# Cosine attention, then a GELU feed-forward, on one core: the opening of the program as one list in another order, and one quad's row sums on VectorE

## The chip, the cores and the metric

One core of a Trainium2 chip. The time is the device time of one execution in microseconds; the kernel before was run three times, at 400.53, 400.88 and 407.3 us, median 400.88. One more execution was recorded by the hardware profiler. Its span, from the first to the last instruction, is 398.6 us; start times below count from the span's start.

The engines are named as the profile names them: PE is TensorE (matmuls; PEld is its weight loading), DVE is VectorE, ACT is ScalarE, POOL is GpSimd, SP is SyncE, which here only issues DMAs. Every engine works through its own instructions in program order and waits on semaphores for the others.

## The reference

Two stages: attention with normalised queries and keys (8 batches, 12 heads, 448 positions, 64 wide), then a feed-forward with exact GELU on the 3584 rows that result (768 to 2048 to 768).

```python
q_n = q / (norm(q, axis=-1) + 1e-06)
k_n = k / (norm(k, axis=-1) + 1e-06)
scores = q_n @ k_n.T / tau                      # tau = 0.1
attn = exp(scores - max)                        # rows divided by their sum
o = (attn / (sum(attn, axis=-1) + 1e-09)) @ v
x = o.transpose(0, 2, 1, 3).reshape(3584, 768)
h = x @ w_in
out = (0.5 * h * (1 + erf(h / sqrt(2)))) @ w_out
```

Since the rows are normalised, scores lie between -10 and 10 and the kernel subtracts no maximum.

## The kernel before

Everything is done by **quads**: four heads of one batch. A batch has three quads, so quad g belongs to batch g // 3, counted from zero; quad 3 is the first of the second batch. A quad's two head pairs are indexed s, its seven chunks of 64 keys c. The preparation of a quad is a **unit**; quad 0 is split into units 0 and 1 (one head pair each), so for later quads unit u is quad u - 1.

The steps of a quad, each a small function in the kernel:

- `load_qk(g)`: q and k from HBM, two DMAs on SP's queue; a pool of four tiles. `load_v`, `load_wi` and `load_wo` load v, w_in and w_out on POOL's queue and turn them into bfloat16 on the way.
- `square`, `reduce`, `logs`, `roots`, `inverses`: the reciprocal norms. Squares on ACT or POOL, sums along a row on DVE, a square root on ACT as logarithm and exponential, the reciprocal on DVE.
- `scale`: q and k times their reciprocal norm, to bfloat16, on POOL.
- `transposes`: the scaled tile turned, by seven PE transposes into PSUM with a DVE copy behind (`copies`) in the opening, later by one DMA transpose on SP's queue.
- `scores(g, banks, p)`: key-by-query scores of two chunks (or of one chunk for both head pairs) in a pair of PSUM banks, four matmuls of 64x64. `exps`: their exponential on ACT, 128x896. `visit(p)` is the next scores and exponential in line, on PSUM pair p.
- `sums(g)`: the row sums of the probabilities as matmuls with ones. `folded` and `gathered` do the same for other quads as additions of the chunks on POOL or DVE; `turned_all` and `inverted_all` finish them with DVE transposes. `turned`, `inverted`: the same for `sums`. `spread`: the reciprocal sums laid out along the rows.
- `values(g)`: probabilities times v. `normalise`: times the spread reciprocals, into x, the input of the feed-forward, one of its six column blocks per call.
- `w_in`: one of the sixteen projection tiles hp of a batch, six matmuls of 128x128 on 448 columns, one for each column block of x; then GELU on ACT into g. Quad 2's `normalise` writes the last two of the six blocks.
- `second_pieces`: the matmuls of the output tiles op, handed out one by one ("pieces", sixteen to a tile) between the scores of the next batch; a DVE copy and a store end each tile.

The order of the instructions is written out by hand for each engine at once: the functions are called in the order wanted, with `tc.manual_schedule()`. `attention_first` is the list for batch 0, `first(b)` the projections of batch b, `attention(b, fill)` the attention of batch b with the output pieces of the batch before (`run()` hands out as many as `parts` says). `upto(f, n)` calls a loading or preparing step up to number n. `spin(n)` issues n matmuls that nobody reads, into the bank that the next tile will take.

ACT holds one set of functions at a time: logarithm and exponential in one, GELU in another; a table load stands between them. PSUM has eight banks: two or three pairs for scores, values and projections (`ps_st`, `third`), two single ones that alternate (`ps_mm`, `mm_tile`), and during batch 0 two more for sums and values (`ps_acc`).

One copy only orders the loads: `late` is a copy on POOL that reads the last element of quad 0's k, so that POOL's loads of v and w_in are issued after quad 0 has landed.

Of the kernel before, what the change touches and what calls it, by code (L numbers as in the profile page):

```python
# [9 lines left out]
F32 = mybir.dt.float32  # L10
# [6 lines left out]
def kernel(  # L17
# [246 lines left out]

    def gathered(g, p):
# [58 lines left out]
    def values(g, chunks=range(C), p=None):  # L324
        for c in chunks:
            if c == 0 and g < NQ:
# [70 lines left out]
    def second_pieces(sb, t, ni):  # L397
        state = {}

        def mm(kf):  # L400
# [8 lines left out]
            if kf == KF - 1:  # L409
                nc.vector.tensor_copy(ot[:, ni * NH:(ni + 1) * NH], ps[:, :NH])  # L410
# [7 lines left out]
        return [lambda kf=kf: mm(kf) for kf in range(KF)]  # L418
# [46 lines left out]
    early = {}  # L465

# [5 lines left out]
    def attention_first():  # L472
        x_t[0] = xp.tile([128, KD, S], BF16, tag="x", name="x0")
        DV, AC, GP = nc.vector, nc.scalar, nc.gpsimd
        Q, K = 0, 1
        square(0, ((AC, Q),))
        square(0, ((AC, K),))
        reduce(0, Q)
        reduce(0, K)
        square(1, ((AC, Q),))  # L480
        upto(load_v, 1)
        logs(0)
        reduce(1, Q)
        roots(0)
        upto(load_wi, 1)
        square(1, ((AC, K),))
        inverses(0)
        square(2, ((AC, Q),))
        reduce(1, K)
        scale(0, ((GP, 1),))  # L490
        logs(1)
        reduce(2, Q)
        roots(1)
        scale(0, ((GP, 0),))
        spin(2)
        transposes(0, 1)
        square(2, ((AC, K),))
        inverses(1)
        spin(1)
        transposes(0, 0)  # L500
        square(3, ((AC, Q),))
        copies(0, 1)
        scale(1, ((GP, 0),))
        copies(0, 0)
        square(3, ((AC, K),))
        scale(1, ((GP, 1),))
        upto(load_qk, 5)
        spin(1)
        transposes(1, 0)
        reduce(2, K)  # L510
        scores(0, ((0, 0), (0, 1)))
        upto(load_v, 2)
        transposes(1, 1)
        copies(1, 0)
        logs(2)
        scores(0, ((0, 2), (0, 3)))
        roots(2)
        upto(load_wi, 2)
        exps(0, ((0, 0), (0, 1)))
        inverses(2)  # L520
        copies(1, 1)
        exps(0, ((0, 2), (0, 3)))
        spin(2)
        scores(0, ((0, 4), (0, 5)))
        scale(2, ((GP, 0),))
        reduce(3, Q)
        exps(0, ((0, 4), (0, 5)))
        spin(1)
        scores(0, ((1, 0), (1, 1)))
        reduce(3, K)  # L530
        exps(0, ((1, 0), (1, 1)))
        spin(1)
        scores(0, ((1, 2), (1, 3)))
        scale(2, ((GP, 1),))
        upto(load_qk, 6)
        transposes(2, 0)
        exps(0, ((1, 2), (1, 3)))
        sums(0, (0,))
        copies(2, 0)
        scores(0, ((1, 4), (1, 5)))  # L540
        logs(3)
        scores(0, ((0, 6), (1, 6)))
        roots(3)
        transposes(2, 1)
        exps(0, ((1, 4), (1, 5)))
        inverses(3)
        sums(0, (1,))
        scale(3, ((GP, 0),))
        copies(2, 1)
        sums(0, (2,))  # L550
        exps(0, ((0, 6), (1, 6)))
        sums(0, range(3, 5))
        scores(1, ((0, 0), (1, 0)))
        scores(1, ((0, 1), (1, 1)))
        sums(0, (5,))
        exps(1, ((0, 0), (1, 0)))
        sums(0, (6,))
        upto(load_wi, 3)
        transposes(3, 0)
        turned(0)  # L560
        exps(1, ((0, 1), (1, 1)))
        scores(1, ((0, 2), (1, 2)))
        values(0, (0,))
        scale(3, ((GP, 1),))
        upto(load_wi, 4)
        copies(3, 0)
        values(0, (1,))
        exps(1, ((0, 2), (1, 2)))
        values(0, (2,))
        scores(1, ((0, 3), (1, 3)))  # L570
        inverted(0)
        values(0, range(3, 5))
        spread(0, 1)
        values(0, (5,))
        exps(1, ((0, 3), (1, 3)))
        scores(1, ((0, 4), (1, 4)))
        values(0, (6,))
        spread(0, 0)
        sums(1, (0,))
        square(4, ((GP, K),))  # L580
        exps(1, ((0, 4), (1, 4)))
        sums(1, (1,))
        scores(1, ((0, 5), (1, 5)))
        normalise(0, 0)
        transposes(3, 1)
        exps(1, ((0, 5), (1, 5)))
        scores(1, ((0, 6), (1, 6)))
        copies(3, 1)
        sums(1, (2,))
        square(4, ((GP, Q),))  # L590
        square(5)
        upto(load_wo, 2)
        exps(1, ((0, 6), (1, 6)))
        sums(1, range(3, 5))
        normalise(0, 1)
        scores(2, ((0, 0), (1, 0)))
        sums(1, (5,))
        exps(2, ((0, 0), (1, 0)))
        sums(1, (6,))
        scores(2, ((0, 1), (1, 1)))  # L600
        turned(1)
        values(1, range(2))
        exps(2, ((0, 1), (1, 1)))
        values(1, (2,))
        scores(2, ((0, 2), (1, 2)))
        inverted(1)
        values(1, range(3, 5))
        spread(1, 0)
        values(1, (5,))
        exps(2, ((0, 2), (1, 2)))  # L610
        values(1, (6,))
        scores(2, ((0, 3), (1, 3)))
        sums(2, (0,))
        reduce(4, K)
        normalise(1, 0)
        exps(2, ((0, 3), (1, 3)))
        sums(2, (1,))
        scores(2, ((0, 4), (1, 4)))
        spread(1, 1)
        values(2, (0,))  # L620
        sums(2, (2,))
        exps(2, ((0, 4), (1, 4)))
        scores(2, ((0, 5), (1, 5)))
        normalise(1, 1)
        values(2, range(1, 3))
        exps(2, ((0, 5), (1, 5)))
        values(2, (3,))
        scores(2, ((0, 6), (1, 6)))
        exps(2, ((0, 6), (1, 6)))
        reduce(4, Q)  # L630
        spin(1)
        early[4] = mm_tile("hp0_4")[:, :S]
        w_in(0, early[4], 4, range(2))
        sums(2, range(3, 7))
        values(2, (4,))
        logs(4)
        turned(2)
        values(2, (5,))
        roots(4)
        values(2, (6,))  # L640
        inverted(2)
        inverses(4)
        scale(4)
        spread(2, 1)
        spread(2, 0)
        normalise(2, 1)
        normalise(2, 0)
        done.update({square: 6, reduce: 5, root: 5, scale: 5, transposes: 5})

# [49 lines left out]

    def attention(b, fill):
        fill = list(fill)
        if b == 1:
            parts = iter((20, 13, 14, 17, 16, 16))
        elif b == 2:
            parts = iter((22, 12, 12, 13, 11, 13, 11, 11, 11, 6, 6))
        elif len(fill) == 128:
# [31 lines left out]
        if b == 1:  # L740
            upto(scale, u + 3)
            upto(load_v, b + 2)
            upto(transposes, u + 3)
            upto(load_qk, g0 + NQ + 2)
            upto(square, u + 4)
            visit(0, 1, 2)
            run()
            visit(0, 1, 2)
            run()
            upto(load_qk, g0 + NQ + 3)  # L750
            visit(0, 1)
            upto(square, u + 5)
            run()
            visit(0, 1, 2)
            both(g0, 0)
            upto(load_v, b + 3)
            upto(load_qk, g0 + NQ + 4)
            visit(1, 2)
            upto(reduce, u + 4)
            run()  # L760
            visit(1, 2, 0)
            both(g0 + 1, 1)
            visit(2, 0)
            logs(6)
            roots(6)
            run()
            both(g0 + 2, 2)
            inverses(6)
            done[root] = 7
        elif b == 2:  # L770
            upto(scale, u + 3)
            upto(load_qk, g0 + 6)
            upto(transposes, u + 3)
            upto(scale, u + 4)
            upto(load_qk, g0 + 7)
            upto(transposes, u + 4)
            visit(0, 1, 2)
            run()
            visit(0, 1, 2)
            norms(9)  # L780
# [230 lines left out]
```

## Time and profile before

| what | value |
|---|---|
| three runs | 400.53, 400.88, 407.3 us; median 400.88 |
| the profiled execution | span 398.6 us, mean granted PE clock 0.999 |
| busy | PE 392.0, POOL 250.6, DVE 264.0, ACT 267.8 us |
| first transposes of quad 0 on PE | 8.65 us |
| exponentials of quads 0, 1, 2 | 12.29 to 31.22 us, 21 of them |
| projections of batch 0 | 32.65 to 51.33 us, with 14 transposes of quad 3 between |
| attention of batch 1 with the output pieces of batch 0 | 51.33 to 79.15 us |
| projections of batch 1 | 79.15 to 97.44 us |
| attention of batch 2 | 97.44 to 133.45 us |
| loads of quads 4 and 5 issued on SP | 11.29 and 16.60 us |
| DMA transposes of quads 4 and 5 issued on SP | 46.34 and 51.47 us |

A busy time is the time in which an engine had an instruction in work; PE's instructions overlap, so a busy PE isn't one at its peak. The chain of waits goes back from the last instruction: at each step to what released it, or to the instruction before it on the same engine. In a row of a timeline the first number is the start, the second the length, then engine, line, operation, output and inputs, shape and count; in brackets stands the idle time before it and who ended it.

### The profile page before, as it was taken

How to read it: one execution, taken by the hardware profiler on the slowest of the kernel's cores; microseconds unless marked ns; L12 is line 12 of the kernel's file. 1: busy time of each engine (PE TensorE's matmuls, PEld its weight loads, DVE VectorE, ACT ScalarE, POOL GpSimd, SP SyncE). 2: the span in 40 equal slices, each digit the busy share in tenths (PEclk: the TensorE clock that was granted, in tenths of full speed). 3: DMA queues.
4: the chain of work that ended last, by engine and by line, in shares of the span. 5: the costliest groups of instructions: out<-in, count | busy, mean ns of one | idle time of the engine just before them, and what ended most of it. 6: DMA issues, size and time to landing. Idle time of an engine off the chain costs nothing.

```text
span 398.6 us, 8027 instructions
## 1 busy us (share of the span) xinstructions
PE 392.0 (98%) x3245; PEld 207.8 (52%) x3245; DVE 264.0 (66%) x530; ACT 267.8 (67%) x399; POOL 250.6 (63%) x162
## 2 busy tenths in 40 slices
PE   7999999999999999999999999999999999999996
PEld 3444555555545555555555555555555555555564
DVE  5787214955487999589963999769973797461021
ACT  6995787557988877888665977889656756504300
POOL 5898814269699694959587394969768391920000
PEclk9999999999999999999999999999999999999999
DMA  8999999747296890678145591566024720130033
GB/s 290 261 258 217 205 233 308 154 106 226 50 254 234 158 230 2 178 150 207 70 105 138 126 240 38 162 113 147 2 27 101 148 46 2 41 77 3 1 80 80
DMA packets 66485, 54.52 MB, mean 137 GB/s; under 512 B 38672, under 2 KB 62352, under 8 KB 66448
## 3 DMA queue, kind: packets, MB, share of 16 engines
q1 hardware_dynamic: 54464, 41.79, 39.0%
q0 software_dynamic: 11600, 11.80, 18.8%
q8 instruction: 25, 0.41, 0.4%
q10 hardware_dynamic: 384, 0.43, 0.3%
q14 instruction: 12, 0.10, 0.1%
HBM read 45.61 MB, written 11.01 MB: 142 GB/s over the span
## 4 chain that ended last, share of the span: by engine, by line
PE 95%; issue 1%; DVE 1%; POOL 1%; ACT 0%; POOLq 0%
PE hp L469 37%; PE op L406 36%; PE st L242 9%; PE o L320 4%; PE o L335 4%; PE op L425 1%; PE sm L305 1%; PE sh L667 1%; PE tp L221 1%; PE sm L314 1%; PE spin L463 0%; POOL wi L441 0%; DVE nq L168 0%; POOL qkb L204 0%; POOL v L145 0%
## 5 line engine op out<-in xcount | busy, mean ns | idle before, releaser
L252 ACT ACTIVATE pt<-st 128x896 bf16<-128x896 f32 x155 | 132.5, 916 | 29.0 <-PE st L242 28.4
L406 PE MATMUL op<-wo,g 128*128 128x384 bf16 x864 | 148.1, 326 | 0.0
L469 PE MATMUL hp<-x,wi 128*128 128x448 bf16 x768 | 147.0, 353 | 0.1
L204 POOL TENSOR_TENSOR qkb<-qk,rn 128x896 bf16<-128x896 f32 (+1 forms) x50 | 80.2, 1628 | 66.3 <-DVE rn L188 64.9
L406 PEld LDWEIGHTS <-g 128*128 128x128 bf16 x864 | 81.4, 98 | 62.6 <-issue 11.2
L469 PEld LDWEIGHTS <-wi 128*128 128x128 bf16 x768 | 74.4, 98 | 71.1 <-issue 2.8
L263 POOL TENSOR_TENSOR acc<-acc,pt 128x896 f32<-128x896 f32 x55 | 103.8, 1887 | 4.3
L929 ACT ACTIVATE g<-hp 128x448 bf16<-128x448 f32 x128 | 63.6, 552 | 63.6 <-PE hp L469 63.5
L410 DVE COPY ot<-op 128x384 f32<-128x384 f32 x54 | 29.9, 555 | 83.1 <-PE op L406 80.8
L168 DVE TENSOR_REDUCE nq<-sq 128x14 f32<-128x896 f32 (+1 forms) x50 | 50.6, 1038 | 10.2 <-POOL sq L160 6.7
L242 PE MATMUL st<-qkT 64*64 64x448 bf16 x620 | 46.0, 356 | 0.2 <-ACT pt L252 0.2
L160 POOL TENSOR_TENSOR sq<-qk 128x896 f32<-128x896 f32 x18 | 29.9, 1683 | 16.3 <-DMA qk<-in_q_dram 10.9
L369 DVE TENSOR_TENSOR x<-o,rs 128x448 bf16<-128x448 f32 x48 | 28.0, 609 | 9.9 <-PE sh L667 6.4
L270 DVE TENSOR_TENSOR acc<-acc,pt 128x896 f32<-128x896 f32 x30 | 33.0, 1099 | 1.0
L158 ACT ACTIVATE sq<-qk 128x896 f32<-128x896 f32 (+1 forms) x32 | 27.8, 902 | 2.2 <-DMA qk<-in_q_dram 1.8
L364 DVE STREAM_TRANSPOSE rs<-rc 128x448 f32<-128x448 f32 x48 | 28.7, 626 | 0.6
L242 PEld LDWEIGHTS <-qkT 64*64 64x64 bf16 x620 | 17.9, 105 | 20.5 <-issue 12.7
L263 POOL TENSOR_TENSOR acc<-pt 128x896 f32<-128x896 bf16 x11 | 20.7, 1879 | 8.9 <-DVE x L369 8.9
L320 PE MATMUL o<-pt,v 64*64 64x448 bf16 x364 | 24.2, 351 | 0.0
L673 ACT ACTIVATE pt<-sh 128x448 bf16<-128x448 f32 x26 | 14.1, 544 | 9.2 <-PE sh L667 8.5
L276 DVE STREAM_TRANSPOSE ta<-acc 128x448 f32<-128x448 f32 x32 | 18.5, 617 | 0.2
L335 PE MATMUL o<-pt,v 64*64 64x448 bf16 x308 | 17.5, 351 | 0.5 <-DVE x L369 0.5
(54 smaller groups left out, 212.4 us busy)
## 6 DMA issues: line engine op xcount, KB each, us to landing
qk<-in_q_dram SPq DMA_DIRECT2D x23, 448.0 KB, 4.6
qk<-in_k_dram SPq DMA_DIRECT2D x23, 448.0 KB, 5.4
out_dram<-ot SPq DMA_DIRECT2D x48, 192.0 KB, 3.2
v<-in_v_dram POOLq DMA_DIRECT2D x7, 672.0 KB, 7.7
wo<-in_moe_w_out_dram POOLq DMA_DIRECT2D x4, 768.0 KB, 11.6
wi<-in_moe_w_in_dram POOLq DMA_DIRECT2D x4, 512.0 KB, 14.4
out_dram<-ot SPq DMA_DIRECT2D x12, 96.0 KB, 2.1
wi<-in_moe_w_in_dram POOLq DMA_DIRECT2D x4, 256.0 KB, 14.6
```

Source lines behind the costliest of these rows:

```text
L160: eng.tensor_tensor(sq, t, t, ALU.mult)
L168: nc.vector.tensor_reduce(nq_t[n][:, j, i], sq_t[g, i][:, s0:s1], mybir.AxisListType.X, ALU.add)
L204: eng.tensor_tensor(qkb[:, i, :, s0:s1].rearrange("p c s d -> p s c d"), t[:, i, s0:s1], rn[:, i].to_broadcast([128, s1 - s0, C, D]), ALU. ...
L242: nc.tensor.matmul(st[cols, n, :S], lhsT=qkT[rows, 1, c, cols], rhs=qkT[rows, 0, :, cols], start=True, stop=True, tile_position=(64 * s, 6 ...
L252: nc.scalar.activation(pt, st[:, :, :S], AF.Exp, scale=inv_tau)
L263: nc.gpsimd.tensor_tensor(acc_t[g], all_t[g][:, 0] if c == 1 else acc_t[g], all_t[g][:, c], ALU.add)
L270: nc.vector.tensor_tensor(acc_t[g], acc_t[g], all_t[g][:, c], ALU.add)
L320: nc.tensor.matmul(bank_t[g, h][64 * s:64 * (s + 1), :S], lhsT=v_t[g][rows, s, c, :], rhs=pt_t[g, s, c][rows], start=(c == 0), stop=(c == ...
L335: nc.tensor.matmul(bank_t[g, h][cols, :S], lhsT=v_t[g][rows, s, c, :], rhs=pt_t[g, s, c][rows], start=(c == 0), stop=(c == C - 1), tile_po ...
L406: nc.tensor.matmul(ps[:, :NH], lhsT=g_t[sb][:, kf, t * 128:(t + 1) * 128], rhs=wo[:, kf, ni * NH:(ni + 1) * NH], start=(kf == 0), stop=(kf ...
L469: nc.tensor.matmul(t, lhsT=wi[:, kd, m * 128:(m + 1) * 128], rhs=x_t[b][:, kd, :], start=(kd == 0), stop=(kd == KD - 1))
L929: nc.scalar.activation(g_t[sb][:, m, hf * S:(hf + 1) * S], hps.pop(m), AF.Gelu)
```

## The change

`attention_first`, `attention(1)`, `attention(2)`, `first(0)`, `first(1)` and the calls ahead of them become one list, `opening()`, from the first load to the end of the attention of batch 2. `first(2)` and everything behind it stay as they were. The helpers hand out projection matmuls by tile and range of column blocks (`mm`), give a tile its PSUM bank apart from its matmuls (`bank`, `bank_o`, `banks`), issue one GELU (`gelu`), and hand out output pieces with the engine that copies the tile out (`run(n, AC)` puts that copy on ACT).

- The squares of unit 1's q, on ACT before, are on POOL; four more squares of 128x896 are on ACT instead of POOL. Seven halves of output tiles are copied out by ACT instead of DVE.
- `load_qk(4)` and `load_qk(5)` are issued on ACT's queue, behind the GELU table load.
- The row sums of quad 3 (batch 2's first, counted from one) are six DVE additions (`gather`) into a tile of the pool of squares, and `turned_all`, `inverted_all`, instead of 16 matmuls.
- `late_copy` comes after quad 2's values instead of ahead of everything on POOL; v is loaded after unit 1's scaling, the first w_in pair before unit 0's, the next two pairs after quad 2's scaling.
- `values(2)` takes a score pair (1) instead of one single and one `ps_acc` bank.
- Quad 5 is scaled before quad 4.

```diff
-    def load_qk(g):
+    def load_qk(g, queue=None):
...
-                eng = nc.scalar if g == 0 and s0 == 0 and i == 1 else nc.sync
+                eng = queue or (nc.scalar if g == 0 and s0 == 0 and i == 1 else nc.sync)
...
+    def gather(g, c):
+        if c == 1:
+            acc_t[g] = sqp.tile([128, 2, S], F32, tag="sq", name=f"acd{g}")
+        nc.vector.tensor_tensor(acc_t[g], all_t[g][:, 0] if c == 1 else acc_t[g], all_t[g][:, c], ALU.add)
...
-            if c == 0 and g < NQ:
+            if c == 0 and g < NQ and p is None:
...
-                nc.vector.tensor_copy(ot[:, ni * NH:(ni + 1) * NH], ps[:, :NH])
+                (nc.scalar.copy if eng is nc.scalar else nc.vector.tensor_copy)(ot[:, ni * NH:(ni + 1) * NH], ps[:, :NH])
...
+    def bank(b, m):
+        hps_t[b, m] = mm_tile(f"hp{b}_{m}")[:, :S]
+
+    def bank_o(b, m):
+        hps_t[b, m] = ps_acc.tile([128, 512], F32, tag="o", name=f"hp{b}_{m}")[:, :S]
+
+    def banks(b, m, p):
+        st = pair(p, f"hp{b}_{m}")
+        hps_t[b, m], hps_t[b, m + 1] = st[:, 0, :S], st[:, 1, :S]
+
+    def mm(b, m, k0, k1):
+        w_in(b, hps_t[b, m], m, range(k0, k1))
+
+    def gelu(b, m):
+        sb, hf = divmod(b, 2)
+        nc.scalar.activation(g_t[sb][:, m, hf * S:(hf + 1) * S], hps_t.pop((b, m)), AF.Gelu)
...
+    def opening():
+        spin(2)
+        load_qk(0)
+        square(1, ((GP, Q),))
+        table(EXP_SET)
+        square(0, ((AC, Q),))
+        spin(20)
+        square(0, ((AC, K),))
+        reduce(0, Q)
+        square(1, ((AC, K),))
+        load_qk(1)
+        load_qk(2)
+        spin(1)
+        reduce(0, K)
+        logs(0)
+        load_wi(0)
+        reduce(1, Q)
+        spin(1)
+        roots(0)
+        square(2, ((AC, Q),))
+        inverses(0)
+        reduce(1, K)
+        reduce(2, Q)
+        spin(1)
+        spin(1)
+        scale(0, ((GP, 1),))
+        transposes(0, 1)
+        logs(1)
+        roots(1)
+        inverses(1)
+        copies(0, 1)
+        scale(0, ((GP, 0),))
+        transposes(0, 0)
+        square(2, ((AC, K),))
+        copies(0, 0)
+        reduce(2, K)
...
+        logs(2)
+        spin(2)
+        load_v(0)
+        transposes(1, 1)
+        roots(2)
+        scores(0, ((0, 0), (0, 1)))
+        copies(1, 1)
+        exps(0, ((0, 0), (0, 1)))
...
+        bank(0, 1)
...
+        mm(0, 1, 0, 2)
...
+        bank_o(0, 0)
...
+        banks(0, 3, 0)
+        values(2, (0,), 1)
+        normalise(1, 0)
+        exps(2, ((0, 6), (1, 6)))
...
+        table(GELU_SET)
...
+        load_qk(4, AC)
...
+        load_qk(5, AC)
...
+        gelu(0, 3)
+        gelu(0, 2)
...
+        square(5, ((AC, K),))
...
+        gelu(0, 4)
...
+        scale(6, ((GP, K),))
...
+        scale(6, ((GP, Q),))
+        run(3)
+        scale(5, ((GP, K),))
+        scale(5, ((GP, Q),))
+        run(2)
+        transposes(5)
+        run(1)
+        load_wo(3)
+        gather(3, 1)
+        gather(3, 2)
...
+        transposes(6)
+        run(2)
+        run(1, AC)
+        run(3)
+        gather(3, 3)
+        run(1)
+        visit(0)
+        load_v(2)
...
+        turned_all(3)
+        inverted_all(3)
+        spread(3, 0)
...
-    for b in range(B):
-        if b == 0:
-            attention_first()
...
+    opening()
+    assert not todo_t, len(todo_t)
+    first(2)
+    for b in range(3, B):
+        attention(b, output_pieces(b - 1))
+        first(b)
```

More of the change, by code (lines that the diff above doesn't have):

```diff
@@ L470, in w_in @@
                              start=(kd == 0), stop=(kd == KD - 1))
[L472 to L648, printed above, removed]
@@ new lines, in attention @@
+        upto(scale, u + 5)
+        upto(transposes, u + 5)
+        upto(load_qk, g0 + 9)
+        mixed(g0, 0, (1,), (2, 1))
+        squared(u + 6, 0)
+        folded(g0 + 2, range(3))
+        run()
+        for h in range(2):
+            spread(g0 + 1, h)
+        if b + 1 < B:
+            visit(2, 0, 1)
+        else:
+            visit(2, 0)
+            weighted(g0 + 1, 1)
+            visit(2)
+        folded(g0 + 2, range(3, 6))
+        run()
+        for i in range(2):
+            reduced(u + 5, i)
@@ L868, in first @@
         u = (b + 1) * NQ + 1
[L869 to L871 removed]
+        hps = {}
+        pairs = ({2: 2, 4: 1, 8: 2}, {2: 0, 4: 2, 8: 0})[min(b, 3) - 2]
+        ahead = 6
         def mm(m, kds):
@@ L920, in first @@
         for m in range(KF):
-            if b == 0 and m == 8:
-                for i in range(2):
-                    transposes(4, i)
-                    copies(4, i)
             if m >= ahead and (m == 0 or m - 1 not in pairs):
```

749 lines of the change are left out of this document (573 added, 176 removed).

## The prediction

> **What bounds the kernel now.** I read the page first, then the chain of waits in order of time, then TensorE (PE), ScalarE (ACT) and the DMA transposes by themselves.
>
> ```profile
> span 398.6 us, 8027 instructions
> PE 392.0 (98%) x3245; PEld 207.8 (52%) x3245; DVE 264.0 (66%) x530; ACT 267.8 (67%) x399; POOL 250.6 (63%) x162
> ...
> PE 95%; issue 1%; DVE 1%; POOL 1%; ACT 0%; POOLq 0%
> ```
>
> PE carries 95% of the chain. The windows by stage show where it isn't full:
>
> ```profile
> 8.00:10.00 2.00, 1.60 (x17) 0.94 (x15) 1.82 (x4) 1.76 (x3) 2.00 (x3) 1.00 1.05 386
> ...
> 28.00:30.00 2.00, 1.57 (x26) 0.72 (x25) 1.90 (x4) 1.45 (x3) 2.00 (x2) 1.00 1.04 246
> ```
>
> From 32 us on PE is busy in the whole of every window until the tail (the first number after the length; DVE, ACT, POOL are the third to fifth). So the change can act in three ways only: when the dense stretch starts, how much PE work it holds, and new holes in it. The opening itself goes at ACT's pace:
>
> ```profile
> 12.16 0.23 ACT L180 ACTIVATE root<-lq 128x28 f32<-128x28 f32 x1
> 12.29 4.13 ACT L252 ACTIVATE pt<-st 128x896 bf16<-128x896 f32 x5
> ...
> 18.66 10.29 ACT L252 ACTIVATE pt<-st 128x896 bf16<-128x896 f32 x12 [0.16 <-PE st L242]
> 29.49 1.73 ACT L252 ACTIVATE pt<-st 128x896 bf16<-128x896 f32 x2 [0.55 <-PE st L242]
> ```
>
> The 21 exponentials of quads 0 to 2 run from 12.29 to 31.22. Twelve in a row take 10.29 us, 0.857 each; 21 are 18.0, one logarithm and root between them 0.5 (16.28 to 16.79), the rest, 0.4, is waits. PE's spare 5.8 us in the opening (spins and holes) can't be used faster than ACT gives probabilities.
>
> PE's own timeline gives the price of a spin:
>
> ```profile
> 1.95 6.35 PE L463 MATMUL spin<-g,ident 128*128 128x448 bf16 x22 [1.95 <-DVE root L92]
> 8.65 0.58 PE L221 MATMUL tp<-ident,qkb 128*64 128x128 bf16 x7 [0.35 <-POOL qkb L204]
> 9.16 0.36 PE L463 MATMUL spin<-g,ident 128*128 128x448 bf16 x1
> 9.58 0.55 PE L221 MATMUL tp<-ident,qkb 128*64 128x128 bf16 x7
> ```
>
> 22 spins take 6.35 us. A spin whose follower waits for its end costs 0.42 (9.16 to 9.58), against 0.19 in a stream (chain: 46 projections in 8.81).
>
> **Opening (price: when the dense stretch starts).** The new list puts 26 spins, not 22, ahead of the first transposes, and by the instruction order of the built kernels the last four are tiles of their own on one PSUM bank, each waiting for the one before, the transposes for the last. 2 and 20 end streaming at about 7.9 to 8.3; four more at 0.42 put the first transposes at about 10.0, against 8.65. Their input is ready earlier than before: the first scaling no longer stands behind a v load (POOL 5.60), only behind half a square and the w_in pair, so at 6.95 instead of 7.63; that gain is lost behind the spins. Then two copies at 0.54 (10.6, 11.14), the reduction (11.7, 1.05), logarithm and root (12.8, 0.48): first exponential 13.28, before 12.29. Adding 18.0 and 0.5: last one ends 31.8, before 31.22. After it, before had 8 sums and 12 values to do (32.65). Now quad 2's first six value chunks wait for the last exponential but one (their PSUM pair), and only 4 values and 4 sums follow the last: about 0.8 us after it, 32.6. Net **0.0**. Bounds: if a waiting spin costs 0.19 and VectorE's order binds (copies from 9.05, third square's end 11.5), exponentials start at 12.1 and the stretch at 31.4, so −1.2; if ACT also meets the old 0.4 of waits and a little more, +0.6.
>
> The "three projection tiles begun early" are mostly names: three tiles get their PSUM early, but only two matmuls (tile 1) stand before quad 2's last exponentials, as many as before (30.55, x2). Worth nothing; the cover for the normalising chain (3.3 us: 0.65+0.33+0.65+0.65+2x0.56 from 32.01 on) is 18 projections, 3.4 us, as before, now with 0.1 to spare. Taken at zero.
>
> **Row sums of quad 3 (batch 2's first).** 16 matmuls leave PE: **−0.78** (65.54 in the chain, x16). VectorE gets six additions of 128x896 and the transposed reduction. The nearest row is the same addition from PSUM, 33.0/30 = 1.10 each, so 6.6 (from SBUF not shown; between 0.6, the 448-wide products' row, and 1.9, POOL's addition: 3.6 to 11.4), plus 4.7 for the rest (128.57 to 133.7 without the copies between, and a spread). VectorE works 1.12 of the 10 us from 52 to 62, so from 55.4 it ends at about 66.7. The normalising after it lets scores into its PSUM pair at 68.9; PE gets there at 69.3. Zero at 1.1 an addition; at POOL's 1.9 it would be +4.4, a far end that I count with the slow cases.
>
> **Loads of quads 4 and 5.** They leave SP at 11.29 and 16.60 for ACT's queue, behind the GELU table, at about 33.6 to 35.0: 4x0.47 of ACT's issue time in a gap that is 3.98 long before the first GELU, so free. Behind the square that waits for quad 4's k on ACT stand the GELUs that free PSUM. PE needs the third GELU at about 40.25, so k must be in by 38.85, 4.8 after its issue. Unhurried loads land in 4.4 to 5.4. Take **+0.1**, bounds 0 to 0.65.
>
> **Transposes and weights at 52 to 66.** GpSimd now scales quad 5 before quad 4, and two w_out loads come first. Hp tile 7 ends at 42.6, GELU, table and logarithm at 45.1, rn at 46.0, four scalings at 1.66: 52.6; then quad 4's DMA transpose, before at 46.34. PE ends the projections at 51.3 as before (94 of them and the transposes: 18.7), then 9 output pieces (0.162 each), 12 scores 0.69, 15 pieces, 12 scores, 12 pieces, 4 scores: 58.8, where quad 4's scores need it: 6.2 us of room. How long does one take?
>
> ```profile
> 46.34 3.58 SPq L216 DMA_TRANSPOSE qkT<-qkb  x1
> ...
> 51.47 8.08 SPq L216 DMA_TRANSPOSE qkT<-qkb  x1
> ```
>
> ```profile
> DMA to landing us min/median/max: 3.4/3.5/12.3
> ```
>
> 8.3 (the first, beside GpSimd's loads at 204 GB/s) and 12.3 (the second, with quad loads ahead in its queue) are the first two; 3.5 the later ones. At 52.6 the three w_out loads (2.36 MB from about 41 at 204 GB/s) are just through, so I take it nearer 3.5: no stall; 8.3 would be +2.1. [...] The row beside a load says 8.3, so by the row it would be 2.1.
>
> The last w_out quarter (issued 52.6, 10.4 as the second pair took) lands at 63.0, where its piece comes; v of batch 2, behind it (54.3, 11.3 as before), lands at 65.6, quad 3's values come at 65.0: **+0.6**. Behind these on POOL stands nothing that PE needs soon; on SP, the next quad's loads. Bounds of both together 0 and 2.1.
>
> **ACT's extra work.** Seven output copies (0.55 each) and three squares move to it, about 7 us over 55 to 134, where it is fullest at 98 to 134 (33.3 of 36); there it gains three copies and loses a square, 0.7 of 2.7 spare: **+0.1**, bounds 0 to 0.4.
>
> Sum: 0.0 − 0.78 + 0.1 + 0.6 + 0.1 = 0.0 against the span of 398.6; what lies around the span is 400.88 − 398.6 = 2.3, so the profiled execution stands as the median: **400.9**. Its own range is −2.0 to +3.0.
>
> **Rivals.** *Faster, 398.9*: spins cost nothing extra and no load is late: −1.2 − 0.78. For it: the earlier scaling; against: the 0.42 rows.
>
> *Slower: quad 4's transpose takes the 12.3 us of the second old one* (late w_out and v share the engines): it lands at 64.9, PE stands 6.1 at 58.8. From a landing 6.2 after issue it decides. 400.9 + 6.1 − 0.6 (v's wait falls inside) = 406.4. Against it: no quad loads ahead in its queue. [...]
>
> *Quad 4's k lands as the first 60 us had it, in 11.3*: at 45.3; with square and GELU (0.93+0.47) PE stands from 40.25 to 46.7: +6.5 for the 0.1, 407.3; at 8.1, as q landed, +3.3: 404.1. Against: by 33.6 the w_in loads (2.1 MB from 21 at 204 GB/s) are through.
>
> **Numbers.** Forecast 0.56, faster 0.18, transpose rival 0.16, late k 0.10. 2% is 8.0 us, about what a measurement of this kernel tells from no change: under 392.9 nothing above leads (0.01); over 408.9 only the far ends of the slow rivals (0.04); within 0.95. Range 398.6 to 404.6: from the faster rival, with the 0.3 between two of the runs, to the forecast's upper bound and a little of the milder slow cases; their far halves (0.13) and some of the faster (0.04) are left out.
>
> **What would show it.** First transposes at 10.0 and first exponential near 13.3 (12.1: the faster rival); last of 21 near 31.8; no 16 sums near 65; PE without holes from 32.6 to 51; a hole before quad 4's scores tells the transpose rival, a hole between the projections near 40 the late k; ones before piece 57 or quad 3's values the w_out and v terms. Wrong in whole if the dense stretch starts over 1 us away from 32.6, or if holes stand after 80, where I see none.

## The result, and the profile after

The kernel with the change takes 410.26 us (median of six, 409.62 to 413.5) against 400.98 for six runs of the kernel before: a ratio of 1.0243, 95% interval 1.0207 to 1.0279. It is slower by more than 2%; the forecast was 400.9, range 398.6 to 404.6. For reading what follows: in the profiled executions of nine of the edited kernels (e5, e9, e10 and e12 to e17) k of quad 1 lands 1.4 to 7.6 us later than in after and ScalarE waits for it in the opening, and the ratios leave out only executions more than 1.5% above the fastest of the same kernel.

The profiled execution has a span of 408.4 us, 9.8 more than before. The head of its page, the granted clock and the chain:

```profile
span 408.4 us, 8009 instructions
PE 395.4 (97%) x3228; PEld 209.1 (51%) x3228; DVE 270.0 (66%) x534; ACT 273.4 (67%) x409; POOL 244.7 (60%) x159
...
PEclk9799998999999999999999999999999999999999
...
PE 75%; POOL 8%; DVE 5%; ACT 4%; issue 4%; DMA 3%; POOLq 0%; DVEq 0%
```

PE has 17 instructions fewer and is busy 3.4 us longer: part of its work went at a lower clock (the 7 and the 8 in PEclk, the slices of 10.2 to 20.4 and 61.3 to 71.5 us), and the chain now holds 8% of POOL and 3% of a DMA. What PE waited for, from the view of waits (in total, times, longest):

```profile
PE st L242 <- DMA qkT<-qkb: 3.6, 1, 3.6
...
PE st L242 <- DVE x L374: 0.8, 1, 0.8
PE st L242 <- ACT pt L252: 0.7, 2, 0.4
PE hp L472 <- ACT g L501: 0.5, 2, 0.3
PE hp L472 <- DVE ot L415: 0.4, 1, 0.4
```

Where the 9.8 come from, by the starts of PE's stages in the timelines of both:

| PE reaches | before | after | later by |
|---|---|---|---|
| projections of batch 0 | 32.59 | 34.95 | 2.36 |
| attention of batch 1 | 51.25 | 53.94 | 2.69 |
| end of the projections of batch 1 | 97.37 | 104.89 | 7.52 |
| projections of batch 2 | 133.38 | 141.38 | 8.00 |
| projections of batch 3 | 176.49 | 185.99 | 9.50 |
| end | 398.6 | 408.4 | 9.8 |

Three steps make most of it: the opening (2.4), the stretch around quad 4's scores (4.8), and what comes between 105 and 186 us (2.0). The opening, by windows of PE (busy time and instructions, granted clock, DMA share, GB/s), after first, and then the kernel of experiment e3, which is the same but for four spins:

```profile
12.00:14.00 2.00, 1.59 (x19) 1.00 1.05 245
14.00:16.00 2.00, 1.44 (x14) 0.79 1.03 232
16.00:18.00 2.00, 2.00 (x13) 0.50 1.15 265
...
20.00:22.00 2.00, 2.00 (x13) 0.51 0.26 38
```

```profile
12.00:14.00 2.00, 2.00 (x21) 1.00 1.05 241
14.00:16.00 2.00, 1.95 (x17) 1.00 1.03 236
16.00:18.00 2.00, 1.85 (x24) 1.00 1.14 262
```

From 15.2 to 22.0 PE runs at half clock. A "busy" PE hides it: in 16 to 18 it is busy throughout with 13 instructions, where e3 does 24. What came just before, in PE's timeline of after:

```profile
13.70 0.56 PE L242 MATMUL st<-qkT 64*64 64x448 bf16 x4 [0.41 <-ACT pt L252]
14.51 0.57 PE L242 MATMUL st<-qkT 64*64 64x448 bf16 x4 [0.24 <-ACT pt L252]
```

The second step is one hole, in the chain of after and in PE's timeline behind it:

```profile
50.15 4.98 POOL qkb L204 x3
55.13 0.02 issue
55.14 10.28 DMA qkT<-qkb
```

```profile
65.46 0.57 PE L242 MATMUL st<-qkT 64*64 64x448 bf16 x8 [3.60 <-DMA qkT<-qkb]
65.97 3.69 PE L411 MATMUL op<-wo,g 128*128 128x384 bf16 x12
```

Quad 4's transpose is issued at 55.14 and lands 10.3 us later; PE stands 3.60. The twelve output matmuls behind it then take 3.6 us in place of 1.94 (12 x 0.162): half clock again.

The third step has two holes in it, in PE's timeline of after; in before PE has neither:

```profile
168.24 0.57 PE L242 MATMUL st<-qkT 64*64 64x448 bf16 x8 [0.84 <-DVE x L374]
...
185.99 4.32 PE L472 MATMUL hp<-x,wi 128*128 128x448 bf16 x22 [0.39 <-DVE ot L415]
```

### The profile page after: what moved, and what is told of

Same layout as the page of the kernel before. It is cut to its first block, busy times and chain, and to the rows that moved or that the text cites. A ratio compares the mean times of both kernels' runs of the same rounds, so it can differ in the third digit from the quotient of the medians.

```text
span 408.4 us, 8009 instructions
## 1 busy us (share of the span) xinstructions
PE 395.4 (97%) x3228; PEld 209.1 (51%) x3228; DVE 270.0 (66%) x534; ACT 273.4 (67%) x409; POOL 244.7 (60%) x159
## 4 chain that ended last, share of the span: by engine, by line
PE 75%; POOL 8%; DVE 5%; ACT 4%; issue 4%; DMA 3%; POOLq 0%; DVEq 0%
PE op L411 28%; PE hp L472 26%; PE st L242 7%; POOL acc L263 6%; PE o L325 4%; PE o L340 3%; DMA qkT<-qkb 3%; POOL qkb L204 2%; PE spin L468 2%; PE sm L310 1%; PE op L430 1%; ACT L480 1%; ACT pt L252 1%; ACT g L501 1%; DVE nq L168 1%
## 5 line engine op out<-in xcount | busy, mean ns | idle before, releaser
L411 PE MATMUL op<-wo,g 128*128 128x384 bf16 x864 | 150.8, 329 | 0.0
L415 DVE COPY ot<-op 128x384 f32<-128x384 f32 x47 | 26.1, 555 | 73.6 <-PE op L411 71.4
L168 DVE TENSOR_REDUCE nq<-sq 128x14 f32<-128x896 f32 (+1 forms) x50 | 50.7, 1037 | 20.5 <-POOL sq L160 16.9
L242 PE MATMUL st<-qkT 64*64 64x448 bf16 x620 | 47.5, 363 | 5.3 <-DMA qkT<-qkb 3.6
L160 POOL TENSOR_TENSOR sq<-qk 128x896 f32<-128x896 f32 (+1 forms) x15 | 24.4, 1632 | 26.3 <-DMA qk<-in_q_dram 21.3
L158 ACT ACTIVATE sq<-qk 128x896 f32<-128x896 f32 (+1 forms) x35 | 31.3, 919 | 3.8 <-DMA qk<-in_q_dram 2.1
L325 PE MATMUL o<-pt,v 64*64 64x448 bf16 x364 | 24.2, 351 | 0.0
L524 ACT ACTIVATE pt<-sh 128x448 bf16<-128x448 f32 x26 | 14.1, 543 | 10.1 <-PE sh L518 9.4
## 6 DMA issues: line engine op xcount, KB each, us to landing
wo<-in_moe_w_out_dram POOLq DMA_DIRECT2D x4, 768.0 KB, 10.4
```

Source lines behind the costliest of these rows:

```text
L158: eng.activation(sq, t, AF.Square)
L168: nc.vector.tensor_reduce(nq_t[n][:, j, i], sq_t[g, i][:, s0:s1], mybir.AxisListType.X, ALU.add)
L242: nc.tensor.matmul(st[cols, n, :S], lhsT=qkT[rows, 1, c, cols], rhs=qkT[rows, 0, :, cols], start=True, stop=True, tile_position=(64 * s, 6 ...
L325: nc.tensor.matmul(bank_t[g, h][64 * s:64 * (s + 1), :S], lhsT=v_t[g][rows, s, c, :], rhs=pt_t[g, s, c][rows], start=(c == 0), stop=(c == ...
L411: nc.tensor.matmul(ps[:, :NH], lhsT=g_t[sb][:, kf, t * 128:(t + 1) * 128], rhs=wo[:, kf, ni * NH:(ni + 1) * NH], start=(kf == 0), stop=(kf ...
```

## The experiments

Each edit is against the kernel with the change ("after"), unless it says "before". The spans of before beside them were mostly 398.6 to 399.6. The openings differ from one execution to the next: the same 26 spins take from 7.45 us (e8) to 8.97 (e6), so the first transposes come between 9.46 and 10.98, and the projections of e2 start 1.0 later than those of after. A single span is read with that in mind. In the names of the code unit 6 is quad 5 and unit 5 quad 4.

**e3: four spins back in the opening.** The kernel before had them between its transposes and scores.

```diff
+        spin(2)
         scores(0, ((0, 0), (0, 1)))
...
+        spin(1)
...
+        spin(1)
         transposes(2, 1)
```

> Changed kernel with four unread matmuls put back into PE's idle stretches between 13 and 15.4 us (two, one and one). Theory (PE's holes there, 1.3 us in all, let the clock fall to half from 15.3 to 21.9 us, and that is what the opening lost): the granted clock stays 1.00, seven transposes take 0.50 instead of 0.93, the last of the 21 exponentials ends near 32.2 instead of 34.09, the projections start at 33.0 to 33.4 instead of 34.95, span 406.5 to 407. Rival (the new order itself is slower, the clock only follows): the projections still start after 34.5 and the span stays at 408 or more.

Span 406.1, 2.3 less; clock 1.00 all through the opening (windows above); projections of batch 0 at 32.69, where after has 34.95 and the prediction 32.6. The hole of 3.50 at quad 4 and the half clock behind it stay. The first step is the spins.

**e4: before, with its four spins at 12.5 to 14.9 taken out.**

> Kernel before without its four unread matmuls between 12.5 and 14.9 us (two, one and one). Theory (short holes there halve the clock): the granted clock falls to 0.50 near 15 us for 3 to 7 us, the projections start 1.5 to 2.5 us later than 32.65, span 400 to 401 instead of 398.6. Rival (only the changed kernel's denser set of holes, or its phase, does it): clock 1.00 throughout, projections at 32.5 to 32.8, span 398.3 to 398.8.

Span 401.5, 2.9 more; the clock falls at the same place, and the projections start at 35.47:

```profile
12.00:14.00 2.00, 1.20 (x11) 1.00 1.14 268
14.00:16.00 2.00, 1.61 (x12) 0.80 1.06 248
16.00:18.00 2.00, 2.00 (x16) 0.50 1.05 238
```

Before has its four spins there and keeps the full clock (PE's share is the first after the length, then PEld, DVE, ACT and POOL, then the clock):

```profile
12.00:14.00 2.00, 1.78 (x12) 0.56 (x11) 1.80 (x5) 1.97 (x5) 2.00 (x4) 1.00 1.12 266
14.00:16.00 2.00, 2.00 (x19) 0.91 (x18) 1.92 (x3) 2.00 (x3) 2.00 (x2) 1.00 1.03 242
16.00:18.00 2.00, 2.00 (x25) 1.01 (x23) 1.56 (x4) 1.97 (x5) 0.88 (x2) 1.00 1.10 248
```

So the cause is the missing activity, in either order of the opening. The other profiles in which quad 1's k comes in time agree: without the spins the clock is halved (e1, e2, e6: seven transposes of 128x128 take 0.93), with them it isn't (e7, e8, e11, e18: they take 0.55 or 0.56).

**e2: the last w_out quarter and v behind the transposes** (moved from 55 us to behind quad 6's square of q).

```diff
-        load_wo(3)
...
-        load_v(2)
...
         square(7, ((GP, Q),))
+        load_wo(3)
+        load_v(2)
```

> Changed kernel with the last quarter of w_out and v of batch 2 loaded only after the two DMA transposes (behind a GpSimd square that waits for q of quad 6). Theory (the two loads beside it stretch the transpose): it is issued at about 55.1 as before and lands 3.5 to 5 us later, by 60; no hole before quad 4's scores at 61.9. The price is a new wait at output piece 57, near 66, for the w_out quarter that is issued about 63 and takes about 10: 5 to 7 us, so the span gains nothing (408 to 410). Rival (the two transposes, issued one behind the other, stretch each other, whatever else is loaded): the first still lands about 10 us after issue and the hole stays at 3 us or more.

Span 412.3, over the 408 to 410 expected; the opening is 1.0 later here. The price was paid elsewhere, as expected (PE waits 5.4 at the piece that needs the quarter). The transposes' own rows answer the question (the time that each issue holds SP, shortest, median and longest in ns, with the first and last start; then from issue to landing):

```profile
L216 SPq DMA_TRANSPOSE qkT<-qkb x2: 1547/1573/1599, 56.2 to 57.9; - x2
...
DMA to landing us min/median/max: 3.6/3.6/3.7
```

With no load beside them, they land in 3.6 and 3.7 where after takes 10.3 and 15.1.

**e1: quad 4 scaled ahead of quad 5**, as before.

```diff
-        scale(6, ((GP, K),))
+        scale(5, ((GP, K),))
...
+        scale(6, ((GP, K),))
+        scale(6, ((GP, Q),))
```

> Changed kernel with quad 4 scaled before quad 5 on GpSimd (only the order of four instructions). Theory (the transpose is late because its input is late): quad 4's DMA transpose is issued at about 51.9 us instead of 55.14; even with the 10.28 us to landing seen in the changed kernel it lands at 62.2, so the hole of 3.60 us before quad 4's scores shrinks to 0.3 or less, the half clock behind it (1.7 us) goes with it, and the span falls from 408.4 to about 403.1. Rival (the landing is set by GpSimd's loads of w_out and v and comes when they are through): it still lands at 64 to 65, the hole stays above 2 us, span 406 or more.

A miss: span 410.1. The transpose leaves at 52.34, lands in 8.3, and the hole before quad 4 is gone; the wait only moved to the weights: the quarter now takes 14.1 us to land and v 17.5.

```profile
PE op L411 <- DMA wo<-in_moe_w_out_dram: 3.0, 1, 3.0
...
PE o L340 <- DMA v<-in_v_dram: 0.8, 1, 0.8
```

**e5: e1, with the last quarter and v issued right behind the third quarter.**

> Changed kernel with quad 4 scaled before quad 5, and with the last quarter of w_out and v of the second batch issued on GpSimd right behind the other w_out loads, ahead of the scalings (about 46 to 48 us instead of 55 to 57). Theory (all these loads and transposes share DMA engines that are full from 44 to 72; what was wrong is that the two loads were issued 8 to 9 us later than they could be): quad 4's transpose lands by 62, the w_out quarter by 65, v by 70; no hole of PE between 54 and 76 over 0.5 us, no half clock there; span 408.4 - 3.6 - 1.7 = 403.1, give or take 0.6 for the start of the clock. Rival (the engines have no room anywhere before 70, so one of the three is late in any order): holes of 2 us or more in all remain, span 405.5 or more.

A miss: span 412.9. Four loads stand in POOL's queue by 50 us; the transpose, issued at 54.97, lands after 15.2 and the hole is 5.13. The projections start 3.2 later than in after, behind the late k of quad 1.

**e15: quads 4 and 5 loaded early on SP's queue** (`load_qk(4)` and `(5)` without `AC`), nothing else.

> Changed kernel with one thing undone: q and k of quads 4 and 5 on SP's queue early, nothing else. Theory (the late q and k loads are half of the backlog): the three w_out quarters issued at 40 to 46 are through by 53 instead of 56, quad 4's transpose, issued about 55 as before, shares the engines only with the last quarter and v and lands in 6 to 8; hole 0 to 1.5 instead of 3.6, half clock gone, span 403 to 405. Rival (only what is issued beside the transpose matters, not what went before): hole of 3 us or more, span 408.

Span 410.3, its projections 0.7 later: the transpose still takes 10.0 and the hole is 3.37, though the DMA engines' busy share was only 0.23 from 36 to 40 us and 0.33 from 40 to 44 (after: 1.00 and 0.69). So the rival holds: the backlog ahead of the transpose isn't the cause, what is under way beside it remains.

**e9: the first two w_out quarters before quad 3's scaling** (near 34 us; after has them at 40.4 and 44.6, because POOL's list puts them behind a scaling that waits for rn until 35.3), the other two and v behind.

```diff
+        load_wo(0)
+        load_wo(1)
...
-        load_wo(1)
+        load_wo(2)
...
-        load_wo(0)
+        load_wo(3)
...
-        load_wo(2)
+        load_v(2)
...
-        load_wo(3)
...
-        load_v(2)
```

> Changed kernel with the loads of w_out and of v of the second batch issued earlier on GpSimd, where it stood idle from 28 to 35: two quarters at about 28 us (before: 30.0; changed: 40.4 and 44.6), a third at about 41, the fourth and v at about 45; quad 5 still scaled before quad 4. Theory (the DMA engines are full from 44 to 72 because w_out comes 10 us later than in the kernel before, while they had room from 20 to 36; the transposes wait behind that backlog): quad 4's transpose, issued about 55, lands in 3.5 to 6 us, by 61.5; the hole of 3.60 and the half clock behind it go, no w_out or v wait appears; span 408.4 - 3.6 - 1.7 = 403.1 (up to 403.8 where the start comes later). Rival (the transposes are slow of themselves when two are issued back to back): hole of 2 us or more before quad 4's scores, span 406 or more.

Span 417.8, 5.84 of it the late k of quad 1. The transposes land in 3.7 and 3.8, no hole at quad 4; but q and k of quads 4 and 5, still issued on ACT's queue from 40.1 to 41.6, now take up to 12.3 to land, and PE waits 2.23 at 50.7 for a GELU that stands behind the square of quad 4's k. This is the prediction's third rival, called up by moving weights. Another 2.22 at 83 is the additions' (below).

**e6: the root and reciprocal of the norms of quads 11 and 12 ahead of quad 8's reciprocal sums**, the order of before. (`roots` and `inverses` count groups of units; group 10 is units 12 and 13.)

```diff
+        roots(10)
+        inverses(10)
         inverted_all(8)
         spread(8, 0)
         run(1)
-        roots(10)
-        inverses(10)
```

> Changed kernel with the square root and the reciprocal of the norms of units 12 and 13 moved ahead of the last step of quad 8's row sums (five lines of the list in another order, at the end of the second batch after the first). Theory (GpSimd's scalings start at 144.21, 2.8 us after the projections of that batch, where they started 0.2 before them in the kernel before; its additions for the next sums end late, and PE stands 0.84 at 168.24 and 0.39 at 185.6): the scalings start by 142, PE's holes at 168 and 186 go, and the projections of the batch after start 43.1 us after those before them instead of 44.6; span 406.9. Rival (the late step is the square that stands between GpSimd's additions at 130.59, not the order on VectorE): scalings still start after 143.5, holes stay, span 408 or more.

Span 406.9, as expected. POOL's scaling of quads 11 and 12, after and then e6:

```profile
144.21 6.63 POOL L204 TENSOR_TENSOR qkb<-qk,rn 128x896 bf16<-128x896 f32 x4 [6.17 <-DVE rn L188]
```

```profile
142.10 6.63 POOL L204 TENSOR_TENSOR qkb<-qk,rn 128x896 bf16<-128x896 f32 x4 [4.01 <-DVE rn L188]
```

It starts 2.8 us behind the projections of batch 2 in after, 0.9 in e6, 0.2 ahead of them in before. With it go the holes of 0.84 at 168 and 0.39 at 186: 1.5 us of the tail.

**e7 and e11: before, with quad 3's row sums as the six additions.** In e7 they stand in one block after eleven visits, in e11 two early and four behind the next visits.

```diff
-            both(g0, 0)
+            for c in range(1, C):
+                gather(g0, c)
+            turned_all(g0)
+            inverted_all(g0)
+            weighted(g0, 0)
```

> Kernel before with one part of the change alone: the row sums of quad 3 by six VectorE additions and the transposed reduction, in place of 16 matmuls. Theory (the term of the row sums holds: 0.78 us less on PE, VectorE has the room): span 397.8, time ratio 0.998. Rival (the additions hold up VectorE's output copies and the normalising, as they stand in one block): a hole of 1 to 3 us between 65 and 75, ratio 1.001 to 1.006.

> Kernel before with quad 3's row sums as VectorE additions, now each placed behind the exponentials that it needs (from about 56 us) and the reduction right behind them, done near 66. Theory (what cost 12 us in the run with the additions in one block was only their place: they began at 65.7, the normalised block was due at 71.5 and came at 80.9): the sums leave PE 0.78, no hole between 60 and 82, span 397.8, ratio 0.998. Rival (VectorE's output copies between the additions are late and hold PE): holes of 0.3 to 1.5 us near 59 to 66, ratio 1.000 or more.

Both missed: ratios 1.0293 (1.0233 to 1.0354) and 1.0168 (1.0119 to 1.0217). In e7 the block ends at 79 and PE waits 9.2 for the normalising behind it; in e11 it waits 5.3 for an output copy behind it. So "-0.78" is the work that leaves PE; whether it arrives in the time depends on what stands behind the additions on VectorE. In both, one addition or more took 2.4 to 2.5 in place of 1.09.

**e8: e5 with e3's spins and e6's order.**

> Changed kernel with all of it together: the four unread matmuls in the opening, quad 4 scaled before quad 5, the last w_out quarter and v issued early, the norms of units 12 and 13 ahead of quad 8's sums. Theory (the four causes add up): 408.4 - 2.3 - 5.3 - 1.5 = 399.3 of span, about 401.3 of time, ratio to before 1.001. Rival (once they are gone other waits of the new order come in their place): span above 402.

A miss, for e5's reason: ratio 1.0200 (1.0137 to 1.0263), the transpose 15.9 from issue to landing. **e10: e9 with the same two.**

> The same with the four unread matmuls in the opening and the norms of units 12 and 13 ahead of quad 8's sums. Theory (the three causes add up): 408.4 - 5.3 - 2.3 - 1.5 = 399.3 of span, ratio to the kernel before 1.001 (0.999 to 1.004). Rival (the projections then start at 32.7 instead of 35, so everything behind asks for its transposes 2.3 us earlier and the hole returns): span 401 or more.

Ratio 1.0171 (1.0098 to 1.0245), over the 1.004 expected: the transpose lands in 3.6, quad 4's late k remains (2.1 before a projection), and so does the 2.22 of the additions. **e12** is e10 without the four single spins ahead of the first transposes.

> The kernel of the run before last (three causes mended) without the four unread matmuls that stand alone ahead of the first transposes. Theory (they hold the first transposes back: each takes 0.41 and the last ends at 9.46, when the first scaled half has been there since 8.0): first transposes by 8.6 instead of 9.5, first exponential by 12.1 instead of 12.75, projections 0.4 to 0.7 earlier. Rival (VectorE's third reduction and the next scaling set the pace, not PE): first exponential still at 12.5 or later, projections no earlier; or the missing work lets the clock fall to half and they start 1 us or more later.

Inconclusive: the late k of quad 1 hid it, though the first transposes came at 8.98.

**e13: e10 with quads 4 and 5 loaded early on SP's queue**, that is, spins, w_out, v, k and q, and the order of the norms of quads 11 and 12 mended, and all else of the change kept; **e18** is the same kernel, for another profile.

```diff
-        load_qk(4, AC)
+        load_qk(4)
...
-        load_qk(5, AC)
+        load_qk(5)
```

> Changed kernel with the opening's four unread matmuls, the norms of units 12 and 13 ahead of quad 8's sums, w_out and v issued earlier, and q and k of quads 4 and 5 loaded on SP's queue as soon as their buffers are free (about 12 and 17 us) instead of on ScalarE's behind the exponentials (34 to 40 us). Theory (it is one backlog on the DMA engines: 1.8 MB of q and k moved from 11-25 us to 34-45, and 2.4 MB of w_out 10 us later; mending only the w_out half made k of quad 4 late, PE stood 2.2 in the projections): no hole in the projections, quad 4's transpose lands within 5 us, no hole before its scores. VectorE's additions for quad 3 then run beside GpSimd's squares and the 2.2 us wait for an output copy near 80 stays. Span 408.4 - 5.3 - 2.3 - 1.5 + 2.2 = 401.5. Rival (the early q and k push w_in and v behind, and a wait appears before 36 us): projections start after 33.5, span 403 or more.

> The kernel with all loads as early as before, the four unread matmuls and the norm step mended, once more for a profile: its first was taken in an execution in which k of quad 1 came 3.4 us late. Theory (the opening is then the old one and the additions still collide with GpSimd's squares): clock 1.00 from 10 to 30 us, projections from 32.5 to 32.9, no hole before quad 4's scores near 59, one wait of 2.0 to 2.4 for an output copy near 71, span 399.5 to 401.5. Rival (the collision belonged to that execution): no wait near 71, span 397.5 to 399.

Ratio 1.0016 (0.9978 to 1.0055): the loss is undone as far as can be told, and nothing is won. (The median of e13's ten runs is 402.61 us, of the nineteen of before 400.89.) In e18's profile quad 1's k comes in time and the clock is 0.999; the wait near 71 that was expected isn't there:

```profile
span 399.6 us, 8018 instructions
...
PE 72%; POOL 11%; DVE 6%; ACT 5%; issue 5%; POOLq 0%; DVEq 0%
```

Its stages start at 33.09, 52.08, 134.17 and 177.52, against 32.59, 51.25, 133.38 and 176.49 before: 0.5 from the opening stays, and 0.5 in small waits. Its transposes land in 4.5 and 5.4, with only v beside them. The chain, 95% PE before, is only 72% PE here: for a quarter of the span it now passes through other engines.

**e14: e13 with quad 3's sums on PE again.**

> The same with quad 3's row sums back on PE as 16 matmuls. Theory (the additions only looked free in the changed kernel because PE stood 3.6 us for the transpose and GpSimd had nothing to do meanwhile; beside a GpSimd square one addition takes 2.38 instead of 1.09): 0.8 of PE work comes back, the 2.2 wait goes: span 400.1, 1.4 less than the kernel with the additions. Rival (the wait near 80 has another cause, such as the order of the output copies): span 0.8 more than the kernel with the additions.

Ratio 1.0023 (0.9972 to 1.0074): no difference from e13 that can be told. **e16: e13 with POOL's square of quad 6's q held until the additions are through** (a small copy on POOL reads the sums), **e17** the same without the four single spins ahead of the first transposes.

> The kernel with all loads as early as before (and the four unread matmuls, and the norm step mended), and GpSimd's two squares of quad 6 held back until VectorE's additions for quad 3 are done (a GpSimd copy of one column of their reduction stands ahead of them). Theory (an addition takes 2.38 instead of 1.09 while GpSimd squares): all five additions 1.09, the reduction ends 2.6 us earlier, the wait of 2.22 for an output copy near 77 is gone; ratio to before 0.996 to 0.999 (1.0016 without it). Rival (the squares held back come too late for quad 6's norms, and a wait appears in the projections of the second batch): ratio 1.002 or more.

> The same without the four unread matmuls that stand alone ahead of the first transposes. Theory (each takes 0.41 and they end 1.5 us after the first scaled half is there): in undisturbed executions the first transposes come at 8.3 to 8.8 instead of 9.5 and the projections 0.3 to 0.7 earlier; ratio 0.001 to 0.002 below the run before it. Rival (the exponentials wait for k of quad 1 and VectorE, not for PE): no difference, or 0.5 to 2 us more if the clock falls to half without them.

They tested a reading of e13's profile, in which quad 1's k is late: two additions beside two POOL squares took 2.4 each, and PE then waited 2.2 (shortest, median and longest addition in ns):

```profile
L268 DVE TENSOR_TENSOR acd<-acd,pt x5: 1092/1092/2381, 63.5 to 69.6; 128x896 f32<-128x896 f32 x5
```

Both missed: ratios 1.0077 (1.0045 to 1.011) and 1.0079 (1.0029 to 1.0129), so leaving out the four single spins shows no gain either. With the square held back all additions take 1.09, but POOL's next square, which waits for its k, ends at 92 us, a normalising stands behind its reduction, and PE waits 2.3 at 95 (2.0 at 88 in e17). And in e18, where nothing was held, additions and squares meet only in the last 0.3 us:

```profile
L268 DVE TENSOR_TENSOR acd<-acd,pt x5: 1092/1092/1092, 57.5 to 62.3; 128x896 f32<-128x896 f32 x5
```

The collision belonged to the execution with the late k: there the additions came 6.0 us later than in e18, the squares only 3.3 (66.39 and 63.14).

## Why the prediction was wrong, step by step

- **Opening, "net 0.0": wrong by 2.4.** The start was priced about right: first transposes at 9.50 (forecast 10.0), first exponential at 12.75 (13.28), within what one execution differs from the next. The failed step is that everything behind was priced at full clock, and the spins that the change removes between transposes and scores were counted as spare ("PE's spare 5.8 us in the opening"). Without them the clock halves from 15.2 to 22.0, PE rather than ACT sets the pace (ACT waits 0.30, 0.93 and 1.24 for scores), and the last exponential ends at 34.09 in place of 31.8. e3 and e4 show it from both sides (-2.3, +2.9), and with the spins the forecast's own number comes out: 32.69 for 32.6. (The cover for the normalising is mis-added: 0.65+0.33+0.65+0.65+2x0.56 is 3.4, not 3.3, so nothing is to spare; PE doesn't wait there in after.)
- **The clock.** Behind the 3.60 hole PE runs at half clock for 3.4 us, from 66.35 to 69.75, and loses some 1.7 (twelve output matmuls in 3.6 in place of 1.94). In the opening there is no such hole: the longest one behind the first transposes is 0.41 in after, e1, e2 and e6 and 0.71 in e4, and yet the clock is halved, for 6.8 us in after, e1, e2 and e4 and for 3.4 in e6. What goes with it is how much work PE has in the least busy 3.4 us between 9 and 32 (a window as long as the half clock behind the hole): it is busy for 65 to 72% of them in these five profiles, and for 84% or more in before, e3, e7, e8, e11 and e18, which keep the full clock. Whether that share decides or where the holes lie, no run here separates.
- **Transposes, "nearer 3.5: no stall": wrong by 4.8 in its stage** (hole 3.60, half clock 1.7, waits 0.3, less the 0.78 of the sums). The failed step is "the three w_out loads [...] are just through, so I take it nearer 3.5". They were issued at 40.4, 44.6 and 45.6, and the third landed only at 57.4; above all, the fourth was issued at 55.07 and v at 56.00, the very moment of the transpose (55.14), and the prediction wrote both issues down in its next paragraph without putting them beside the transpose. The room was right (6.7; forecast 6.2). The mechanism was that of the transpose rival (chance 0.16) at a milder size, 10.3 where it took 12.3. Landing by what is under way beside it: nothing, or the last 1.0 us of v, 3.6 to 3.8 (e2, e9, e10); the last 3.6 us of v, 4.5 and 5.4 (e18); the end of the third quarter, the fourth and v, 10.0 to 10.3 for the first transpose (after, e15) and 15.1 to 16.5 for the second, issued right behind it; two quarters and v, all queued ahead, 15.2 and 15.9 (e5, e8). So a transpose took 1.25 (4.5) to 4.6 (16.5) times the 3.6 alone, by how much was queued beside and ahead of it.
- **w_out and v, "+0.6": not seen**, since PE was itself late at both. The quarter took 12.0 to land, v 15.2, longer than the 10.4 and 11.3 assumed: e1, in which PE is not late, pays 3.0 and 0.8 for them.
- **Late k, "+0.1": right** in after, where PE doesn't wait for it; e9 shows that the rival was near. **ACT's extra work, "+0.1"**: one wait of PE for a root on ACT, 0.18 at 120.85.
- **Row sums, "-0.78": right in size.** Six additions of 1.09 (forecast 1.10), done at 65.3, no wait of PE behind them (POOL had nothing to do beside them in after). The bound at POOL's price was real in another form: beside a POOL square one takes 2.4 to 2.5 (e7, e11, e13). That it is worth 0.78 in the time isn't shown: e13 and e14 can't be told apart.
- **"Holes after 80, where I see none": wrong, 2.0.** The list swaps the reciprocal norms of quads 11 and 12 with quad 8's sums; the prediction worked out no place behind 80 us but ACT's total. e6 gives 1.5 of it back.

The faster rival is out: the opening didn't gain. Steps 2.36, 0.33, 4.83, 0.48, 1.50 and 0.3 add up to the 9.8, and mending their causes (e18) takes all but 1.0 of it away. What delays quad 1's k stays open. No kernel here beats the one before.

## What to carry to other kernels

A filler matmul can keep the clock up (e3: 1.00 with four of them back, where after has 0.50): before taking one out, look at what share of PE's last few microseconds is left without it, and not only at the length of the holes, and then check the granted clock rather than the busy share. Price a DMA by what else is under way or issued while it runs, on every queue, on the new timeline and not the old (the same transpose took 3.6 us with no load beside it in e2, and 10.3 in after). And when a list is rewritten, walk each engine's queue to the list's end, since a small swap late in it (a scaling 3 us later on POOL) cost 1.5 us here; a wait that is mended in one place comes up at the next one unless that has room (e1, e5, e9, e16).

## What the hardware showed that was not expected

- Half clock (0.50) without a hole worth the name: 15.2 to 22.0 us in after, behind holes of 0.41 and 0.24 and in one of 0.32.
- A DMA transpose of one quad takes 3.6 us by itself and up to 16.5 beside loads from POOL's queue and behind another transpose, and its issue can hold SP meanwhile: 8.02 in e15, 8.85 in e8, against 1.6 in e2.
- A VectorE addition of two SBUF operands takes 1.09 alone and 2.38 beside a POOL square (e7, e13), which then takes 2.09 in place of 1.68 (e7). The row that the prediction used could not show it: there the accumulator lies in PSUM, and each of its 30 additions took 1.10 with POOL's own additions running beside it (before).
